# Moving a small weight load from the SP queue to the ACT queue, and placing the last adds with their multiplies, in a six-layer cross network

## The chip, the cores and the metric

One core of a Trainium2 chip runs the kernel. The metric is device time in microseconds (us), median of several executions. Times quoted from a profile are counted from the first instruction of the profiled execution, whose span is about 2 us shorter than the time (485.8 us for an execution of 487.98 us). Engines are called PE (TensorE matmul), PEld (its weight load), DVE (VectorE), ACT (ScalarE), POOL (GpSimd) and SP (SyncE, which here only issues DMAs). In the views a q after the name (SPq, ACTq) marks the engine's sequencer, which issues its DMAs; a DMA "lands" when its completion is signalled.

## The reference

```python
B, F, D, L = 16384, 26, 16, 6
Din = min(F * D, 1024)            # 416 = 3*128 + 32
def reference(x0, ws, bs):        # x0 (B, Din), ws (L, Din, Din), bs (L, Din), all bf16
    x = x0
    for l in range(ws.shape[0]):
        x = x0 * (jnp.einsum('bd,de->be', x, ws[l]) + bs[l]) + x
    return x
```

## The kernel before

Features lie on partitions, and a group of 2048 rows is four chunks of 512 columns. The 416 features make three tiles of 128 and a tail of 32. In each layer and group a 128-wide output tile sums, for each of its four chunks, three products with K=128 (`full`) and one with K=32 for the tail features. The four K=32 matmuls of a tile form one group (`rows32`): its weights are `w3`, its moving operand is `x3`, the tail of the previous layer's result. The tail of the output is computed by `tails`. ACT evicts PSUM with the bias (`tw`), DVE multiplies by x0 and adds x (`evacuate`).

The program keeps one list of instructions for each engine, in the order of the calls, except that a DVE add of `evacuate` or `tails` goes behind the next multiply of such a pair where one follows. The helper `add` records what each reads and writes, and puts a semaphore wait where another engine or an earlier DVE instruction made the data. The parts that matter here:

```python
    def load_w3(l, eng):                     # four copies of the K=32 weights of layer l
        for j in range(NJ):
            add(eng, lambda h, j=j: h.dma_start(w3[l][j * T32:(j + 1) * T32, :], ws[l, NT * P:D, :]), ...)

    load_w3(0, "sp"); make_wbd(0)
    load_group(1, lambda: load_wm(1, "sp"))  # four DMA transposes, large weights of layer 1, four copies
    load_w3(1, "sp")                         # <- behind all of these
    load_wm(2, "sp"); load_w3(2, "sp")
    make_wbd(1); make_wbd(2)
    ...
    def first_job():                         # group 0, layer 0: rows are transposed on PE
        ...
        transposed_chunk(3)
        full(g, l, 1, bb, True, True, chunks=[0, 1])
        full(g, l, 0, ba, True, True, chunks=[2, 3])
        rows32(g, l, 0, ba, False)
        evacuate(g, l, 0, ba, [0, 1], 2, vector=[2, 3])
        ...
        full(g, l, 2, ba, False, True, lambda j: evacuate(g, l, 2, ba, [j], 1))
        finish_tile(g, l, NT)
        tails([(g, l)])                      # makes x3 for layer 1, last on DVE's list
```

After the first job PE takes tile 0 of (group 1, layer 0), which ends with its K=32 group, and then tile 0 of (group 0, layer 1), which begins with its K=32 group. The latter is PE's first use of `w3[1]` and of the new `x3`.

The last layer of the last group is computed with rows on partitions, in four row sets `kk`, each with four chunks `j`, so that it can be stored directly:

```python
    def layer_full(kk, bks, ts=range(NT)):
        for j in range(NJ):
            nat_full(kk, j, bks[j], False, ts)   # PE
            nat_mul(kk, j, bks[j])               # ACT copies PSUM, DVE multiplies; the very last: DVE alone
            if j:
                nat_add(kk, j - 1)               # DVE
            if kk == last and j == 2:
                nat_store(kk - 1, kk + 1, 0, 2)  # SP, 416 KB
            if kk == last and j == 3:
                nat_store(kk, kk + 1, 2, 3)      # SP, 104 KB
        nat_add(kk, NJ - 1)
    ...
    layer_full(3, bkb)
    nat_store(3, 4, 3, NJ, "act")                # ACT, 104 KB, the last store
```

## Time and profile before

| | before |
|---|---|
| time, median of the first 3 runs | 487.45 us (487.36 to 488.09) |
| PE busy | 472.8 of 485.8 us |
| PE waits for layer 1's K=32 weights | 1.1 us, once |
| PE's last matmul ends | 481.39 us |
| last add ends, last store's issue | 483.22 us, 483.26 us |

From the page of the kernel before: busy time of the engines, the granted clock in 40 slices, and the chain of work that ended last.

```profile
PE 472.8 (97%) x3199; PEld 203.2 (42%) x3253; DVE 407.2 (84%) x713; ACT 343.2 (71%) x372; POOL 16.0 (3%) x44
...
PEclk9999999999999999999999999999999999999999
...
PE 91%; SPq 4%; ACT 2%; issue 2%; DVE 1%; DMA 0%; DVEq 0%
```

In this profile the records of 54 matmuls are missing (3199 matmuls against 3253 weight loads).

PE is the limit for nearly the whole span, so only time in which PE stands still, or time after its last matmul, can be won without taking away matmuls.

From the list of waits of the kernel before (who waited for whom: us in total, times, longest):

```profile
PEld ps L436 <- DVE x L414: 1.4, 1, 1.4
...
PE ps L436 <- DMA w<-in_ws_dram: 1.1, 1, 1.1
```

L436 is the K=32 group. There are two records for one stall: the matmul's wait is put down to the weights (the DMA), the weight load's to the DVE add that writes `x3` (L414). The timeline of PE and DVE at that place (start us, duration us, engine, line, operation, count, idle time before it and what ended it):

```profile
22.93 0.39 PE L436 MATMUL ps<-x,w 32*128 32x512 bf16 x4
24.41 0.40 PE L436 MATMUL ps<-x,w 32*128 32x512 bf16 x4 [1.09 <-DMA w<-in_ws_dram]
...
22.61 0.76 DVE L397 TENSOR_TENSOR x<-tw,x 128x512 bf16<-128x512 bf16 x2
23.29 0.42 DVE L412 TENSOR_TENSOR ts<-ts,x 128x512 bf16<-128x512 bf16 x1
23.74 0.43 DVE L414 TENSOR_TENSOR x<-ts,x 128x512 bf16<-128x512 bf16 x1
```

And the chain of waits at the same place (start us, us, what):

```profile
22.61 1.66 DMA w<-in_ws_dram
24.27 0.14 issue
24.41 0.40 PE ps L436 x4
```

The weights land at 24.27 us, and the add ends at 24.17 us.

The tail of the kernel before: DVE and ACT in the timeline (L797 multiply, L802 add, L792 the multiply that reads PSUM), then two lines of the DMA issues (queue, size, median us from issue to landing).

```profile
480.93 0.38 DVE L797 TENSOR_TENSOR x<-x,x 128x416 bf16<-128x416 bf16 x1 [0.15 <-ACT x L795]
481.22 0.37 DVE L802 TENSOR_TENSOR x<-x,x 128x416 bf16<-128x416 bf16 x1
481.50 0.37 DVE L797 TENSOR_TENSOR x<-x,x 128x416 bf16<-128x416 bf16 x1
481.79 0.37 DVE L802 TENSOR_TENSOR x<-x,x 128x416 bf16<-128x416 bf16 x1
482.07 0.59 DVE L792 TENSOR_TENSOR x<-ps,x 128x416 bf16<-128x416 f32 x1
482.57 0.65 DVE L802 TENSOR_TENSOR x<-x,x 128x416 bf16<-128x416 bf16 x2
483.26 0.38 ACTq L809 DMA_DIRECT2D out_dram<-x  x1
```

```profile
out_dram<-x SPq DMA_DIRECT2D x1, 416.0 KB, 2.5
...
out_dram<-x ACTq DMA_DIRECT2D x1, 104.0 KB, 2.1
```

A DVE instruction that takes 0.37 us starts 0.28 us after its predecessor when it doesn't need its result. The last store leaves 1.87 us after PE's end and takes 2.1 us.

### The profile page before, as it was taken

The page shows a single profiled execution, that of the slowest core. Times are in us where ns is not written, and L with a number is a line of the kernel's source. Part 1 is how long each engine was busy: PE and PEld are TensorE (multiplying, and loading weights), DVE is VectorE, ACT ScalarE, POOL GpSimd, SP SyncE. Part 2 cuts the span into 40 slices and gives each one's busy share as a digit, 9 for nine tenths or more (in the row PEclk, how much of TensorE's full clock was granted, in tenths as well). Part 3 has the DMA queues.
Part 4 walks back from the last instruction along what each step waited for, and adds up shares of the span by engine and source line. Part 5 has one row for each costly group of instructions (what it writes and reads, how often), then busy time and mean ns, then how long its engine had stood idle before and what let it go on. Part 6 is the DMA issues. An engine that isn't in the chain of part 4 may idle for free.

```text
span 485.8 us, 8047 instructions
## 1 busy us (share of the span) xinstructions
PE 472.8 (97%) x3199; PEld 203.2 (42%) x3253; DVE 407.2 (84%) x713; ACT 343.2 (71%) x372; POOL 16.0 (3%) x44
## 2 busy tenths in 40 slices
PE   8999999999999999999999999999999999999996
PEld 6344444444444444433444444444444444444353
DVE  2778888888888888888888888888888888888887
ACT  4567777677677676767777767767767767777775
POOL 1042100000000000000000000000000000000000
PEclk9999999999999999999999999999999999999999
DMA  9897990000002396269209921850000137027277
GB/s 230 167 168 164 177 185 2 0 1 0 2 1 44 68 241 115 45 150 224 50 15 188 222 44 37 215 173 1 1 1 1 25 67 191 0 45 166 78 161 258
DMA packets 126249, 47.65 MB, mean 98 GB/s; under 512 B 107002, under 2 KB 124804, under 8 KB 126212
## 3 DMA queue, kind: packets, MB, share of 16 engines
q1 hardware_dynamic: 125656, 46.71, 43.5%
q8 instruction: 25, 0.41, 0.4%
q10 hardware_dynamic: 556, 0.43, 0.3%
q14 instruction: 12, 0.10, 0.1%
HBM read 5.97 MB, written 13.63 MB: 40 GB/s over the span
## 4 chain that ended last, share of the span: by engine, by line
PE 91%; SPq 4%; ACT 2%; issue 2%; DVE 1%; DMA 0%; DVEq 0%
PE ps L424 73%; PE ps L436 8%; PE ps L449 6%; PE ps L454 2%; SPq L301 2%; PE ps L767 1%; SPq L287 1%; ACT tw L383 1%; SPq L306 1%; ACT x L795 1%; SPq L313 0%; SPq L479 0%; DMA w<-in_ws_dram 0%; ACT x L759 0%; PE ps L778 0%
## 5 line engine op out<-in xcount | busy, mean ns | idle before, releaser
L383 ACT ACTIVATE tw<-ps,bias 128x1024 bf16<-128x1024 f32 (+1 forms) x295 | 299.8, 1071 | 128.4 <-PE ps L436 105.7
L424 PE MATMUL ps<-x,wm 128*128 128x512 bf16 x1638 | 371.9, 379 | 5.6 <-issue 3.7
L424 PEld LDWEIGHTS ps<-x,wm 128*128 128x128 bf16 x1692 | 158.8, 98 | 213.3 <-issue 28.5
L392 DVE TENSOR_TENSOR tw<-tw,x 128x1024 bf16<-128x1024 bf16 (+1 forms) x285 | 193.8, 686 | 63.4 <-ACT tw L383 63.1
L397 DVE TENSOR_TENSOR x<-tw,x 128x1024 bf16<-128x1024 bf16 (+1 forms) x285 | 182.3, 680 | 0.0
L436 PE MATMUL ps<-x,w 32*128 32x512 bf16 x564 | 44.5, 380 | 1.1 <-DMA w<-in_ws_dram 1.1
L449 PE MATMUL ps<-x,wm 128*32 128x512 bf16 x564 | 38.7, 380 | 0.0
L410 ACT ACTIVATE ts<-ps,bias 128x512 bf16<-128x512 f32 x47 | 28.8, 701 | 0.0
L436 PEld LDWEIGHTS ps<-x,w 32*128 32x128 bf16 x564 | 9.2, 92 | 34.5 <-issue 33.1
L449 PEld LDWEIGHTS ps<-x,wm 128*32 128x32 bf16 x564 | 13.8, 96 | 15.7 <-issue 2.9
L414 DVE TENSOR_TENSOR x<-ts,x 128x512 bf16<-128x512 bf16 x47 | 18.7, 423 | 0.0
L412 DVE TENSOR_TENSOR ts<-ts,x 128x512 bf16<-128x512 bf16 x47 | 18.7, 421 | 0.0
L609 POOL COPY ost<-ot 128x512 bf16<-128x512 bf16 x7 | 4.8, 682 | 411.0 <-DMA ot<-x 411.0
L454 PE MATMUL ps<-x,wbd 128*32 128x512 bf16 x188 | 18.3, 379 | 0.0
L294 POOL COPY wbd<-w 32x32 bf16<-32x32 bf16 x24 | 9.1, 380 | 37.6 <-DMA w<-in_ws_dram 36.5
L767 PE MATMUL ps<-wm,x 128*128 128x416 bf16 x48 | 9.4, 341 | 0.0
L536 DVE COPY x<-ps 128x512 bf16<-128x512 bf16 x4 | 1.7, 424 | 8.3 <-PE ps L528 8.3
L795 ACT ACTIVATE x<-ps 128x416 bf16<-128x416 f32 x15 | 7.4, 530 | 1.3 <-PE ps L767 1.2
L533 ACT ACTIVATE x<-ps 128x512 bf16<-128x512 bf16 x8 | 4.3, 594 | 4.3 <-PE ps L523 4.3
L454 PEld LDWEIGHTS ps<-x,wbd 128*32 128x32 bf16 x188 | 5.0, 97 | 5.1
L767 PEld LDWEIGHTS ps<-wm,x 128*128 128x128 bf16 x48 | 5.1, 115 | 3.7 <-issue 1.4
L797 DVE TENSOR_TENSOR x<-x,x 128x416 bf16<-128x416 bf16 x15 | 5.5, 373 | 1.1 <-ACT x L795 1.0
(37 smaller groups left out, 49.2 us busy)
## 6 DMA issues: line engine op xcount, KB each, us to landing
out_dram<-ost SPq DMA_DIRECT2D x7, 1664.0 KB, 6.8
x<-in_x_dram SPq DMA_DIRECT2D x7, 416.0 KB, 7.4
wm<-in_ws_dram SPq DMA_DIRECT2D x5, 312.0 KB, 3.2
x<-Tb SPq DMA_DIRECT2D x28, 32.0 KB, 2.0
out_dram<-x SPq DMA_DIRECT2D x1, 832.0 KB, 3.6
w<-in_ws_dram SPq DMA_DIRECT2D x24, 26.0 KB, 2.2
x<-in_x_dram SPq DMA_DIRECT2D x2, 208.0 KB, 3.1
out_dram<-x SPq DMA_DIRECT2D x1, 416.0 KB, 2.5
```

The source lines that it names most:

```text
L383: add("act", lambda h, a=a, w=w, b0=b0: h.activation(tw[r][:, a * CH:(a + w) * CH], psum[:, b0 * CH:(b0 + w) * CH], ACT_F.Identity, bias=b ...
L392: add("dve", lambda h, a=a, e=e: h.tensor_tensor(tw[r][:, a * CH:e * CH], tw[r][:, a * CH:e * CH], x0s[s0][:, i * GC + a * CH:i * GC + e * ...
L397: add("dve", lambda h, a=a, e=e: h.tensor_tensor(xs[so][:, i * GC + a * CH:i * GC + e * CH], tw[r][:, a * CH:e * CH], src(i, a, e), ALU.ad ...
L410: add("act", lambda h: h.activation(ts[r][:, :], bank(b), ACT_F.Identity, bias=bias[:, 3, l:l + 1], scale=1.0), reads=[("ps", b), "bias"], ...
L412: add("dve", lambda h: h.tensor_tensor(ts[r][:, :], ts[r][:, :], x0s[s0][:, XW:XW + CH], ALU.mult), reads=[("ts", r)] + x03_toks(s0), writ ...
L414: add("dve", lambda h: h.tensor_tensor(x3s[so][:, :], ts[r][:, :], src, ALU.add), reads=[("ts", r)] + stok, writes=[("x3", so)], hold=True)
L424: add("pe", lambda h, t=t, j=j: h.matmul(bank(banks[j]), wm[l][:, t, ecols], src(t, j, j + 1), start=(first and t == 0), stop=(not first a ...
L436: add("pe", lambda h, q=q, j=j: h.matmul(bank(banks[j]), w3[l][q, ecols], src[q, :], start=first, stop=not first, tile_position=(j * T32, 0)),
L449: add("pe", lambda h, t=t, j=j, src=src, l=l, b=b: h.matmul(bank(b, j * T32, (j + 1) * T32), wm[l][:, t, NT * P:D], src(t, j, j + 1), star ...
L454: add("pe", lambda h, j=j, s3=s3, l=l, b=b: h.matmul(bank(b, j * T32, (j + 1) * T32), wbd[l][:, j * T32:(j + 1) * T32], s3, start=False, s ...
L767: add("pe", lambda h, t=t: h.matmul(bank(b, n=D), xcol(t, j, kk), wm[l][:, t, :], start=(first and t == 0), stop=(not first and t == NT - 1)),
L795: add("act", lambda h: h.activation(o, bank(b, n=D), ACT_F.Copy), reads=[("ps", b)], writes=extra + [("on", j, kk)])
```

## The change

Its intent: the four loads of layer 1's K=32 weights leave the SP queue, where they stand behind the transposes, and are issued by ACT in a stretch where it idles. `make_wbd`, POOL's copies of a corner of these weights into `wbd` for the tail's output, moves along, because it reads them. In the last row set, adds go directly behind their multiplies, so that two of the three last stores can leave earlier.

```diff
     load_group(1, lambda: load_wm(1, "sp"))
-    load_w3(1, "sp")
     load_wm(2, "sp")
     load_w3(2, "sp")
-    make_wbd(1)
-    make_wbd(2)
@@ first_job
         transposed_chunk(3)
+        load_w3(1, "act")
+        make_wbd(1)
+        make_wbd(2)
         full(g, l, 1, bb, True, True, chunks=[0, 1])
@@ layer_full
             nat_mul(kk, j, bks[j])
-            if j:
-                nat_add(kk, j - 1)
-            if kk == last and j == 2:
+            if kk < last:
+                if j:
+                    nat_add(kk, j - 1)
+            elif j == 1:
+                nat_add(kk, 0)
+                nat_add(kk, 1)
                 nat_store(kk - 1, kk + 1, 0, 2)
-            if kk == last and j == 3:
+            elif j == 2:
+                nat_add(kk, 2)
                 nat_store(kk, kk + 1, 2, 3)
         nat_add(kk, NJ - 1)
```

## The prediction

> **What bounds the kernel now.** TensorE: the page has PE busy 472.8 of 485.8 us; the chain of waits gives PE 91% of the span, at a granted clock of 0.999. From about 25 to 466 us matmuls follow one another, and nothing in the diff touches them. Only head and tail can move; both parts of the change are there.
>
> **Head.** The list of waits has one PE wait on a weight load: 1.1 us for layer 1's K=32 weights. In the timeline PE ends a row group at 23.32 us and begins the next at 24.41 us. SP issues these four loads at 21.05 to 23.03 us, after the transposes; the chain has the landing end at 24.27 us. The change issues them on ACT between its last input copy (ends 12.23 us) and its first eviction (14.71 us): 2.48 us idle. Four issues cost 1.98 us on SP here, and 2.51 us for the four copies out of the transposed buffer, so I expect 2.0 to 2.6 us: just fitting, and PE's next use of those banks has some 0.3 us of slack. The weights should land before 20 us.
>
> But the same matmuls have a second input, the tail of layer 0's result. The weight-load engine's wait is put down to the DVE add that writes it, 23.74 to 24.17 us. DVE works without a gap from 17.59 us, fed by the evictions, so this add does not come earlier. With early weights PE starts at about 24.2 us: of 1.1 us about 0.2 us is gained. The later SP loads move some 2 us forward, which gains nothing: no PE wait on DMA follows.
>
> Risk: SP is inside two transposes from 12.80 to 17.82 us. The Trainium skill ("DMA: Bandwidth & Descriptors", section "Issuing engines are not separate DMA queues") says that issuing from several engines saves only the sequencer's issue time, the DMA engines being the same. The trace of before has no ACT issue beside a transpose. If ACT's issues stall behind them, the first eviction starts late and up to some 2 us are lost.
>
> **Tail.** From 480.9 us DVE alternates multiplies with another chunk's adds, mostly 0.28 us a step (timeline); the last add ends at 483.22 us, ACT issues the last store at 483.26 us, landing 2.1 us later, then the end. The new order has as many operations, but adds 2 and 3 directly follow their multiplies: each waits for a full 0.37 us (0.59 us from PSUM) plus about 0.03 us (as the trace's dependent tail multiply and add) instead of 0.28 or 0.50 us. Estimate: last add 0.2 to 0.3 us later. The other two stores go 0.3 us (416 KB) and 0.4 us (104 KB) earlier, but ACT's store is last, so the end moves about 0.2 us later.
>
> **Sum.** About -0.2 us head, +0.2 us tail: 487.5 us, range 486.7 to 488.6. Chances: faster by over 2% 0.005, within 2% 0.985, slower 0.01.
>
> **What would show it.** No PE wait on the weight load; PE waits for the DVE tail add until 24.2 us instead of 24.41; ACT issues between 12.3 and 14.8 us, its first eviction near 14.7; last add 0.2 to 0.3 us later relative to PE's end; ACT's store landing last.
>
> **What would make it wrong.** ACT issues held behind transposes (1 to 2 us slower); the DVE chain moving with the loads; an SP store landing last, so that the tail gains.

## The result, and the profile after

| | before | after |
|---|---|---|
| median of 6 runs | 487.74 us (487.36 to 488.38) | 487.86 us (487.36 to 488.28) |
| span of the profiled execution | 485.8 us | 485.8 us |

The ratio is 1.0000, with a 95% interval of 0.9987 to 1.0013.

Waits of the changed kernel, the two lines that answer to those of before:

```profile
PEld ps L436 <- DVE x L414: 1.2, 1, 1.2
...
PE ps L436 <- DVE x L414: 1.0, 1, 1.0
```

The wait on the weights is gone from PE, and nearly as long a wait for the DVE add stands in its place. The timeline of the changed kernel, PE and DVE, then ACT:

```profile
23.15 0.40 PE L436 MATMUL ps<-x,w 32*128 32x512 bf16 x4
24.50 0.40 PE L436 MATMUL ps<-x,w 32*128 32x512 bf16 x4 [0.95 <-DVE x L414]
...
24.01 0.42 DVE L414 TENSOR_TENSOR x<-ts,x 128x512 bf16<-128x512 bf16 x1
```

```profile
11.37 0.60 ACT L530 ACTIVATE x<-ps 128x512 bf16<-128x512 bf16 x1 [0.67 <-PE ps L520]
11.37 1.25 ACTq L287 DMA_DIRECT2D w<-in_ws_dram  x2
11.86 0.59 ACT L530 ACTIVATE x<-ps 128x512 bf16<-128x512 bf16 x1
12.65 0.93 ACTq L287 DMA_DIRECT2D w<-in_ws_dram  x2
14.94 1.11 ACT L383 ACTIVATE tw<-ps,bias 128x1024 bf16<-128x1024 f32 x1 [2.49 <-PE ps L436]
```

ACT issued the loads between 11.37 and 13.58 us, beside its own last two input copies, and its first eviction still waited 2.49 us for PE, as before (2.48 us). The weights landed by 16.43 us, some 8 us before they are used. The add ends at 24.43 us, and PE starts 0.06 us later.

The tail of the changed kernel, DVE and ACT, and the same two DMA lines:

```profile
481.01 0.38 DVE L797 TENSOR_TENSOR x<-x,x 128x416 bf16<-128x416 bf16 x1 [0.15 <-ACT x L795]
481.31 0.66 DVE L802 TENSOR_TENSOR x<-x,x 128x416 bf16<-128x416 bf16 x2
481.88 0.37 DVE L797 TENSOR_TENSOR x<-x,x 128x416 bf16<-128x416 bf16 x1
482.28 0.37 DVE L802 TENSOR_TENSOR x<-x,x 128x416 bf16<-128x416 bf16 x1
482.57 0.58 DVE L792 TENSOR_TENSOR x<-ps,x 128x416 bf16<-128x416 f32 x1
483.19 0.37 DVE L802 TENSOR_TENSOR x<-x,x 128x416 bf16<-128x416 bf16 x1
483.60 0.37 ACTq L809 DMA_DIRECT2D out_dram<-x  x1
```

```profile
out_dram<-x SPq DMA_DIRECT2D x1, 416.0 KB, 2.5
...
out_dram<-x ACTq DMA_DIRECT2D x1, 104.0 KB, 1.7
```

An add that directly follows its own multiply now starts only after that has ended (481.88 + 0.37 us, then 482.28 us), 0.40 us after it instead of 0.28 us. So the last add ends later against PE's end, 2.08 us instead of 1.83 us. But the last store then takes 1.7 us instead of 2.1 us.

Both kernels have a start-up that differs from execution to execution, by more than the change is worth. It helps to cut the span at three points: A, the start of the last K=32 group before the stall (22.93 us before, 23.15 us after); PE's end; the last landing. Worked out from the recorded start, end and landing times of each profile:

```
                       weights  tail add  next K=32   A to     last add  ACT store  last    end of span
run                A   landed   ended     group at    PE's end ended     issued     landed  after that
                                                               (the last three: us after PE's end)
before          22.93  24.27    24.17     24.41       458.47   1.83      1.87       3.92    0.49
tail_only       23.07  24.40    24.31     24.53       458.44   2.08      2.11       3.81    0.49
tailfirst_old_  23.07  24.30    22.64     24.44       458.35   1.83      1.86       3.92    0.48
after           23.15  16.43    24.44     24.50       458.34   2.08      2.11       3.82    0.49
head_only       22.78  16.71    24.07     24.12       458.32   1.83      1.86       3.92    0.48
late_stores     23.25  16.57    24.51     24.57       458.29   4.42      4.45       6.16    0.48
late_stores2    22.52  16.34    23.81     23.86       458.33   2.09      2.12       4.34    0.49
tailfirst       22.99  16.39    22.60     23.21       457.21   2.08      2.11       3.80    0.49
tailfirst_again 23.35  16.76    22.97     23.58       457.19   2.09      2.12       3.82    0.49
both            23.47  16.64    23.08     23.70       457.19   1.83      1.86       3.63    0.48
both_split      23.56  18.04    23.16     23.78       457.20   1.83      1.86       3.58    0.49
```

(The third row is the run tailfirst_old_load.) Between before and after, A to PE's end shrinks by 0.13 us, and PE's end to the last landing by 0.10 us. The gain of 0.23 us in all is 0.05% of the span. A lies between 22.52 and 23.56 us in these eleven profiles. It differs by 0.36 us between two runs of one file (tailfirst and tailfirst_again), so one profile of each kernel can't tie it to an edit. In the pair before and after it was 0.22 us later in the changed kernel, and that alone hid the gain. Why A moves was not settled; in this pair the shift is there before the moved loads are issued (ACT's third input copy starts at 8.29 us before and at 8.51 us after, the first moved load at 11.37 us).

### The profile page after: what moved, and what is told of

It reads as the page before. It is cut to its first block, busy times and chain, and to the rows that moved or that the text cites. A ratio compares the mean times of both kernels' runs of the same rounds, so it can differ in the third digit from the quotient of the medians.

```text
span 485.8 us, 8101 instructions
## 1 busy us (share of the span) xinstructions
PE 478.7 (99%) x3253; PEld 203.4 (42%) x3253; DVE 407.8 (84%) x713; ACT 343.2 (71%) x372; POOL 16.5 (3%) x44
## 4 chain that ended last, share of the span: by engine, by line
PE 96%; DVE 2%; ACT 1%; POOL 0%; issue 0%; POOLq 0%
PE ps L424 76%; PE ps L436 8%; PE ps L449 6%; PE ps L454 2%; PE ps L767 1%; PE ps L520 1%; PE ps L500 1%; DVE x L397 1%; ACT x L795 1%; DVE tw L392 1%; ACT x L759 0%; PE ps L525 0%; DVE x L802 0%; PE ps L778 0%; ACT tw L383 0%; PE ps L737 0%
## 5 line engine op out<-in xcount | busy, mean ns | idle before, releaser
L424 PE MATMUL ps<-x,wm 128*128 128x512 bf16 x1692 | 379.4, 380 | 0.0
L397 DVE TENSOR_TENSOR x<-tw,x 128x1024 bf16<-128x1024 bf16 (+1 forms) x285 | 182.6, 681 | 0.0
L414 DVE TENSOR_TENSOR x<-ts,x 128x512 bf16<-128x512 bf16 x47 | 18.5, 417 | 0.0
L412 DVE TENSOR_TENSOR ts<-ts,x 128x512 bf16<-128x512 bf16 x47 | 18.5, 417 | 0.0
```

The source lines that it names most:

```text
L397: add("dve", lambda h, a=a, e=e: h.tensor_tensor(xs[so][:, i * GC + a * CH:i * GC + e * CH], tw[r][:, a * CH:e * CH], src(i, a, e), ALU.ad ...
L412: add("dve", lambda h: h.tensor_tensor(ts[r][:, :], ts[r][:, :], x0s[s0][:, XW:XW + CH], ALU.mult), reads=[("ts", r)] + x03_toks(s0), writ ...
L414: add("dve", lambda h: h.tensor_tensor(x3s[so][:, :], ts[r][:, :], src, ALU.add), reads=[("ts", r)] + stok, writes=[("x3", so)], hold=True)
L424: add("pe", lambda h, t=t, j=j: h.matmul(bank(banks[j]), wm[l][:, t, ecols], src(t, j, j + 1), start=(first and t == 0), stop=(not first a ...
```

## The experiments

Theory for the head: PE needs both the weights and the tail add, they end 0.1 us apart, so that hurrying either alone wins next to nothing, and both together about 1.1 us or more. Rivals: the whole stall was the load and the last adds gave the gain back; or only the DVE add mattered; or another wait follows directly. Theory for the tail, formed on seeing the result: the last store's landing waits for the bytes queued ahead of it. Rival: issue plus a fixed time, and 1.7 us was chance.

### Each part alone

head_only is the changed kernel with the old `layer_full`; tail_only is the kernel before with the new one.

> Only the weight-load part of the change. If the DVE tail add is the second input that ends just behind the weights (my theory), PE's wait before layer 1's first K=32 group shrinks from 1.09 us to about 0.95 us and is put down to that DVE add; the DVE end of that add relative to the layer-0 row group before it stays as before. Ratio 0.9995 to 1.0. Rival (the whole wait was the load, and the adds of the last rows gave the gain back): wait near 0.1 us and span about 1 us shorter, ratio 0.998.

Measured: 487.87 us, ratio 1.0007 (0.9995 to 1.0020). The profile has this line:

```profile
24.12 0.39 PE L436 MATMUL ps<-x,w 32*128 32x512 bf16 x4 [0.94 <-DVE x L414]
```

The wait is 0.94 us and not 0.1 us, so the rival (all of it the load) falls. A to PE's end is 458.32 us, 0.15 us less than before. The time cannot show this.

> Only the add placement. DVE's last add ends 0.25 us later relative to PE's last matmul (2.08 instead of 1.83 us after it), ACT's last store is issued that much later. If the SP stores, now 0.3 to 0.4 us earlier, free the DMA engines for it, it lands about 1.7 us after issue instead of 2.1 us and the end does not move: ratio 1.000 within 0.001. Rival (1.7 us was chance): landing 2.1 us, end 0.25 us later, ratio 1.0005.

Measured: 487.97 us, ratio 1.0003 (0.9991 to 1.0016). The last add ended 2.08 us after PE's end, ACT issued at 2.11 us, and the landing was at 3.81 us, 1.70 us after issue:

```profile
out_dram<-x ACTq DMA_DIRECT2D x1, 104.0 KB, 1.7
```

So the 1.7 us was no chance: all profiles with the new add order and early stores have 3.80 to 3.82 us, all with the old order 3.92 us. The part alone brings the end 0.11 us forward.

### The other input alone, and both inputs

The edit, in `first_job`, moves the two DVE instructions of the 32-row tail (L412 and L414) ahead of the last five DVE instructions of the third tile. The instructions are independent of each other.

```diff
         tails([(g, l)])
+        q = pr.queue["dve"]
+        two = q[-2:]
+        del q[-2:]
+        q[-5:-5] = two
```

tailfirst_old_load makes it in the kernel before, tailfirst in the changed kernel.

> The kernel before with only one edit: the two DVE instructions of the first job's 32-row tail go ahead of the last five DVE instructions of its third tile. The tail add ends about 1.7 us earlier (near 22.5 us), but the weights still land near 24.3 us: by my theory PE still waits about 1.1 us, now for the weights alone, and the ratio stays 1.000. Rival (only the DVE add mattered): the wait goes, about 1 us gained, ratio 0.998.

Measured: 487.75 us, ratio 1.0001 (0.9989 to 1.0014). PE's second group, the DVE add and the first POOL instruction that reads the same weights:

```profile
24.44 0.40 PE L436 MATMUL ps<-x,w 32*128 32x512 bf16 x4 [0.97 <-DVE x L397]
...
22.21 0.42 DVE L414 TENSOR_TENSOR x<-ts,x 128x512 bf16<-128x512 bf16 x1
...
24.43 0.98 POOL L294 COPY wbd<-w 32x32 bf16<-32x32 bf16 x2 [12.36 <-DMA w<-in_ws_dram]
```

The add is done at 22.64 us, but PE still starts at 24.44 us, 0.14 us after the weights landed at 24.30 us, as in the kernel before (24.27 us and 24.41 us). The profile names another DVE add (L397) that happened to end then. The group doesn't read that add's result, and the next run, where the same add ends after PE has gone on, shows that it is not what was waited for. The POOL copy, which reads only the weights, starts at the same moment. So the rival (only the DVE add mattered) falls as well.

> The changed kernel with the same DVE edit: both inputs early. By my theory PE goes from one row group to the next with at most 0.1 to 0.2 us idle, 0.9 to 1.0 us gained, and as PE is busy to the end the span gets shorter by that: ratio 0.998. Rival (another wait follows directly, for example the third tile's last chunks that the edit delays by 0.8 us, or layer 1's large weights): PE idles elsewhere in the next 10 us and the ratio stays near 1.000.

Measured: 486.69 us, ratio 0.9980 (0.9967 to 0.9994). PE and DVE in this run:

```profile
22.25 0.81 PE L424 MATMUL ps<-x,wm 128*128 128x512 bf16 x3
22.99 0.61 PE L436 MATMUL ps<-x,w 32*128 32x512 bf16 x8
23.53 1.69 PE L424 MATMUL ps<-x,wm 128*128 128x512 bf16 x7
...
22.17 0.43 DVE L414 TENSOR_TENSOR x<-ts,x 128x512 bf16<-128x512 bf16 x1
...
23.52 0.75 DVE L397 TENSOR_TENSOR x<-tw,x 128x512 bf16<-128x512 bf16 x2
```

The two K=32 groups are now one row of eight matmuls, without a gap, and the large matmuls follow at once. A to PE's end is 457.21 us: 1.26 us less than before and 1.13 us less than after. So no other wait took the place of this one, and the third tile's last chunks, which the edit delays, were still in time.

> The same file as the run named tailfirst, beside the next two on one chip. Again 0.998, about 1 us faster than before, and the last landing 3.80 us after PE's end.

Measured on another chip, beside the runs below: 486.83 us, ratio 0.9975 (0.9962 to 0.9987), A to PE's end 457.19 us, last landing 3.82 us after PE's end. The gain repeats.

The four combinations, in A to PE's end, are 458.47 us (neither input early), 458.34 (weights early), 458.35 (tail add early) and 457.21 (both). Of 1.26 us, neither alone brings more than 0.13 us here (0.15 us with head_only for the early weights). (The 0.12 us of the tail add alone is not even the edit's: PE began 0.14 us after the weights had landed in both runs, and A lay 0.14 us later in a run whose weights landed 0.03 us later.)

### What sets the last landing

> The changed kernel, but the two SP stores of the last rows also wait for a later DVE instruction: the 416 KB store for add 2, the 104 KB store for multiply 3. DVE's order and the ACT store's issue (2.11 us after PE's last matmul ends) stay. If the bytes queued before it set when ACT's store lands (my theory), it lands near 4.3 us after PE's end instead of 3.82, 2.1 to 2.2 us after its issue, and the end is 0.4 to 0.5 us later. Rival (last issue plus a fixed time): it lands at 3.8 us as in the changed kernel.

This run did not test what it was made for: 489.83 us, ratio 1.0040 (1.0026 to 1.0054). To delay the 104 KB SP store I had declared that it reads the last chunk after its multiply; then the last add, which writes that chunk, had to wait for the store's landing:

```profile
485.59 0.38 DVE L802 TENSOR_TENSOR x<-x,x 128x416 bf16<-128x416 bf16 x1 [2.37 <-DMA out_dram<-x]
```

It has a use: ACT's store left at 4.45 us after PE's end, when the other stores had landed (4.02 us), and landed 1.7 us after its issue:

```profile
out_dram<-x ACTq DMA_DIRECT2D x1, 104.0 KB, 1.7
```

So 1.7 us is what 104 KB cost with no other store in the way.

The mended run delays only the 416 KB store, by a read of chunk 2 after its add:

```diff
                 nat_add(kk, 1)
-                nat_store(kk - 1, kk + 1, 0, 2)
             elif j == 2:
                 nat_add(kk, 2)
+                nat_store(kk - 1, kk + 1, 0, 2, after=[("on", 2, kk)])
                 nat_store(kk, kk + 1, 2, 3)
```

> Mends late_stores, where the 104 KB store also read the chunk that add 3 still had to write, so that add 3 waited for the store's landing. Here only the 416 KB SP store is late: it waits for add 2 and goes out 1.20 us after PE's end, the 104 KB one directly behind it at about 1.6 us; DVE's order and waits are those of the changed kernel, ACT's store goes out at 2.11 us. If the queue ahead of it delays its landing (my theory): SP stores land at 3.73 and about 4.05 us, ACT's at about 4.3 us instead of 3.82, the end 0.5 us later. Rival (issue plus 1.7 us whatever is queued): 3.8 us.

Measured: 488.16 us, ratio 1.0006 (0.9990 to 1.0021). The time does not tell it, the landings do: SP's at 3.71 and 4.05 us after PE's end, ACT's at 4.34 us, with its issue at 2.12 us as in the changed kernel.

```profile
out_dram<-x SPq DMA_DIRECT2D x1, 104.0 KB, 2.4
out_dram<-x ACTq DMA_DIRECT2D x1, 104.0 KB, 2.2
```

The same last store, issued at the same moment, lands 0.52 us later because the SP stores ahead of it left later, the 416 KB by 0.69 us (1.20 instead of 0.51 us after PE's end) and the 104 KB behind it by 0.42 us (1.62 instead of 1.20 us). The run moves both, so it tells neither their shares nor whether the bytes or the number of stores matter. The rival falls: the end is not the last issue plus a fixed time. ACT's store comes 0.29 us behind SP's last landing here, and 0.29 us in the kernel before (3.63 us and 3.92 us); in the changed kernel it comes 0.49 us behind and takes the 1.7 us of a store alone.

### A version that beats both

both is the kernel of tailfirst with the multiply that reads PSUM moved ahead of add 2. No add then directly follows its own multiply, while the 416 KB store stays early.

```diff
-            elif j == 2:
+            elif j == 3:
                 nat_add(kk, 2)
                 nat_store(kk, kk + 1, 2, 3)
```

> The kernel of tailfirst with multiply 3 moved ahead of add 2, so that no add directly follows its own multiply, the 416 KB store staying early. DVE's last add ends 1.83 us after PE's end as in the kernel before, not 2.08; ACT issues at 1.86 us and its store lands near 3.6 us instead of 3.8 (tailfirst) or 3.92 (before). About 0.2 us less than tailfirst: ratio 0.9975, which the times alone may not tell from 0.998; the trace will. Rival (the landing is set by the bytes in the queue alone): 3.8 us again.

Measured: 486.58 us, ratio 0.9972 (0.9959 to 0.9984). Its DVE in the timeline:

```profile
480.49 0.65 DVE L806 TENSOR_TENSOR x<-x,x 128x416 bf16<-128x416 bf16 x2
481.06 0.37 DVE L801 TENSOR_TENSOR x<-x,x 128x416 bf16<-128x416 bf16 x1
481.34 0.59 DVE L796 TENSOR_TENSOR x<-ps,x 128x416 bf16<-128x416 f32 x1
481.84 0.65 DVE L806 TENSOR_TENSOR x<-x,x 128x416 bf16<-128x416 bf16 x2
```

PE ended at 480.66 us here. The last add ends 1.83 us after that, as in the kernel before, and the last landing is at 3.63 us, 0.19 us earlier than in tailfirst_again and 0.29 us earlier than before. The times of both and tailfirst_again overlap (486.36 to 486.93 us and 486.36 to 487.01 us), so their difference is shown by the trace alone. Against the kernel before, the time is clearly shorter, though by 0.3% and far from 2%.

both_split also stores the third row set whole, one step earlier, so that 208 KB less are queued after PE's end:

```diff
-                nat_store(kk - 1, kk + 1, 0, 2)
+                nat_store(kk, kk + 1, 0, 2)
...
-    nat_store(2, 3, 2, NJ)
+    nat_store(2, 3, 0, NJ)
```

> As both, but the third row set's first half is stored with its second half one step earlier, so that 208 KB less are queued after PE's end. If ACT's store then meets no queue, its landing is 1.7 us after issue, at 3.55 us after PE's end, nothing or at most 0.1 us less than both. If bytes in the queue are still what it waits for, it gains 0.3 us or more.

Measured: 486.66 us, ratio 0.9970 (0.9955 to 0.9985); last landing 3.58 us after PE's end, 1.72 us after its issue. 0.05 us is gained, and the store now costs what it costs alone, although SP's 104 KB store, issued 0.29 us before it (1.57 and 1.86 us), is still under way. What is left is the end of the last add and the 1.7 us of the store itself.

The traces allow a closer rule than "bytes queued ahead", fitted afterwards, tested by no further run and without a cause shown for its 0.3 us: in all eleven profiles each of the two last 104 KB stores (SP's, then ACT's) lands within 0.05 us of the later of two moments, 1.7 us after its own issue and 0.3 us after the landing of the store before it. In the kernel before the second moment decides (3.63 + 0.3 us against 1.86 + 1.7 us, measured 3.92 us), in the changed kernel the first (2.11 + 1.7 us against 3.33 + 0.3 us, measured 3.82 us).

## Why the prediction was right or wrong

The total was right: 487.5 us with 486.7 to 488.6 us was predicted, and 487.86 us measured, a ratio of 1.000. In part this is luck: the range is far wider than either term, and the tail's term, wrong by 0.3 us, is lost in the scatter of about 1 us. The two terms came out as follows.

- **PE bounds the kernel, and only head and tail can move: right.** From the group after the stall to PE's end the profiles of before and after agree (24.41 to 481.39 us and 24.50 to 481.48 us, both 456.98 us).
- **Of the 1.1 us wait only about 0.2 us is gained, because the DVE add ends just behind the weights: right in mechanism and near in size.** The wait went from 1.09 to 0.95 us, and A to PE's end from 458.47 to 458.34 us. The two-by-two of early weights and early add shows it.
- **"The DVE add does not come earlier": right.** It ended 1.24 us after A before and 1.29 us after A in the changed kernel (24.17 - 22.93 and 24.44 - 23.15 us).
- **ACT's issues fit, between 12.3 and 14.8 us: the outcome was right, the times were not.** They ran from 11.37 to 13.58 us, partly beside ACT's own copies. The prediction let the issues begin only when ACT's last copy had ended. The Trainium skill ("Perfetto Trace Analysis", section "Sequencer Loop") describes a loop in which a sequencer reads the next instruction and pushes it, if it is an engine's, into a queue; this trace agrees in that the issues didn't wait for the copies in front of them to end: the first issue begins at 11.37 us, the very moment at which the first of ACT's last two copies begins, and two are out by 12.62 us, when the second copy (to 12.45 us) has barely ended. What the prediction took from the skill ("DMA: Bandwidth & Descriptors", section "Issuing engines are not separate DMA queues"), that only issue time is saved, the DMA engines being the same, agrees too: SP's large-weight load for layer 2 moved from 23.08 to 20.81 us, which PE did not feel, while the four small loads, now beside SP's transposes, took 3.30 to 3.73 us from issue to landing instead of 1.66 to 1.89 us. With 8 us to spare that did no harm. The feared stall of the issues behind SP's transposes came only in small: the four took 0.32, 0.90, 0.45 and 0.46 us (the second 1.10 us in head_only), and the first eviction was not delayed.
- **"The end moves about 0.2 us later": wrong.** SP's stores did leave 0.28 and 0.38 us earlier, and the last add did end 0.25 us later, as estimated from 0.37 us plus 0.03 us. The step that failed is "landing 2.1 us later", a term carried over unchanged although the same paragraph had the other two stores leave earlier. In the changed kernel that term measured 1.7 us, so that the end came 0.10 us earlier against PE's end instead of 0.2 us later. The runs late_stores2 (4.34 us with a late 416 KB store) and late_stores (1.7 us with none in the way) show why.
- **The sum.** Predicted -0.2 and +0.2 us; measured in the traces -0.13 and -0.10 us. That the median didn't fall by 0.23 us is no contradiction: A moved by +0.22 us between the two profiles, and single executions of either kernel spread over about 1 us, so the times can't show so small a gain.

## What to carry to other kernels

When an engine waits for two inputs, ask for each input when it would have been ready had the other been early: a list of waits gives one name, and it can even be the wrong one (in tailfirst_old_load an add that PE didn't wait for). Here the two inputs came 0.1 us apart, so that neither fix alone won more than 0.15 us and both won 1.26 us. At the end of a kernel count the stores that are still under way ahead of the last one, not only the moment at which it is issued: an earlier big store can pay for a later last one. Where an effect is smaller than the scatter of the start, cut the trace at points that repeat (here PE's end, which lay 458.3 to 458.5 us after A in all kernels with the stall) and compare the pieces.

## What the Trainium skill lacked or had wrong

- "VectorE: DVE Perf Modes", section "The DRAIN you can't avoid", says of a chain of eight tensor_copy that a semaphore after each "costs nothing extra here", and the page's rules advise to minimise the count of instructions, not of semaphores. It does say that a next instruction that is not held starts earlier, but not by how much. Here the wait had a price: a DVE add of 128x416 bf16 that waits for the multiply directly before it starts 0.40 us after that one's start (0.37 us plus 0.03 us), where an instruction that needs nothing of its predecessor starts 0.28 us after it. In the tail two such pairs, one of them reading PSUM, cost 0.25 us (last add 2.08 us after PE's end against 1.83 us), and reordering alone gave it back (both: 1.83 us).
- "DMA: Bandwidth & Descriptors", section "Anatomy of one DMA — SWDGE (gpsimd) path", gives about 2.0 us of fixed cost plus the bytes; its fit is for the GpSimd path (worked out for 104 KB, an estimate, 2.2 us), and the page has no such fit for stores issued from SP and ACT, nor for a store behind others. Here a 104 KB store from ACT landed 1.7 us after its issue with nothing ahead of it, one of 416 KB from SP 2.5 us after, and a 104 KB store close behind two others 2.1 or 2.2 us after.
- "Perfetto Trace Analysis", section "DMA Instruction — HWDGE (DVE, Sync)", has the issuing sequencer wait for a lock on the shared descriptor generator, but gives no figure for an issue on ACT while SP is issuing DMA transposes. Here four such issues took 2.2 us in all (11.37 to 13.58 us; SP's transposes were issued from 9.89 to 12.83 us and from 12.88 us on), and delayed no eviction; the second took 0.90 us and the others 0.32 to 0.46 us, and the loads landed 3.30 to 3.73 us after issue.
